# Splitting each stage of a fused attention and expert kernel into steps per engine, and placing all steps with a list scheduler

## The chip, the cores and the metric

The kernel runs on one core of a Trainium2 chip. The metric is the device time of one execution in microseconds (us); lower is better. Every time given is a median unless it says otherwise. Times inside an execution are counted from the start of the profiled span and come from one profiled execution of each kernel.

In this kernel TensorE does all matrix products and transposes and writes them into PSUM, an on-chip memory used as eight banks. VectorE and ScalarE work on the results; copying a result out of PSUM is called an *eviction*. GpSimd issues the loads. The *granted clock* is the share of its full clock that the profile shows for TensorE; *half clock* means 0.5.

## The reference

Sliding-window causal attention (window 64) over 8 batches, 8 heads, 576 positions, head size 64. Then each batch is averaged over its positions, a gate picks one of 8 experts from the average, and the whole batch goes through that expert's two matrices.

```
scores = (1/sqrt(D)) * q @ k.T            # masked to 0 <= i - j < 64
attn   = exp(scores - max) / sum
x      = (attn @ v), heads side by side   # (8, 576, 512)
pooled = x.mean(axis=1);  e = argmax(pooled @ w_gate)
h      = relu(x @ w1[e])                  # 512 -> 1024
out    = gate_weight * (h @ w2[e])        # 1024 -> 512
```

One consequence governs everything: the expert of a batch is not known before all of that batch's attention is done. Its 4.2 MB of weights (float32 in memory, half that once loaded) can only be asked for after that.

## The kernel before

A batch is five *units*: units 0 to 3 are two heads each over positions 0 to 511, unit 4 is the last 64 positions of all heads. Units are numbered through, so units 0 to 4 are batch 0 and units 5 to 9 batch 1. The expert part of a batch is 18 *chunks*: nine of the first matrix and nine of the second. A string fixes the order in which stages are emitted; each engine then works through its own instructions in that order and waits for what it needs. The stages of a unit (cuts marked `# ...`):

```python
"Q1 L1 t1 T0 T1 U0 S0 U1 E0 S1 K0 T2 U2 S2 T3 E1 M K1 V0 U3 A0 E2 T4 K2 A1 X0 F2 U4 A2 "
"S3 L2 Q2 X1 S4 X2 E3 E4 K3 A3 K4 T5 A4 F2 X3 U5 X4 G0 H0 T6 V1 S5 F4 t2 U6 I0 E5 Q3 K5 "   # ...
"T11 X8 U11 A9 S10 t3 X9 E10 K10 C2 L3 C2 G1 Q4 V2 H1 I1 S11 C1 T12 E11 U12 A10 K11 X10 "   # ...

load_qk(0, 2, 4); load_v(0); load_qk(0, 4, 8); load_tail(0)     # first loads (heads from, to)

def unit_tp(b, i):   # T: 16 transposes of q and k into one PSUM bank (tp)              TensorE
def unit_te(b, i):   # U: copy of q, then copy of k, out of that bank (qt, kT)          VectorE
def unit_s(b, i):    # S: scores into PSUM (s); units 1-4 first add the mask by matmul  TensorE
def unit_e(b, i):    # E: pe = exp(scale * s)                                           ScalarE
def unit_k(b, i):    # K: pe *= mask (not for units 1-4)                                VectorE
def unit_a(b, i):    # A: denominators, products and reciprocals in one stage
    lb = ps_a.tile([128, 4, 128], FP32, tag="lb")
    for hh in range(2):
        nc.tensor.matmul(out=lb[...], lhsT=ones, rhs=pe[:, hh], ...)      # denominators
    for m in range(8):
        for hh in range(2):
            nc.tensor.matmul(out=av[...], lhsT=vt[:, m, 2*i+hh], rhs=pe[:, hh, m], ...)
    nc.scalar.activation(out=ln, in_=lb, func=AF.Ln)
    nc.scalar.activation(out=rl, in_=ln, func=AF.Exp, scale=-1.0)         # 1/denominator
def unit_x(b, i):    # X: x = av * rl, and its sum over positions                       VectorE
def shift_v(b):      # V: v moved between partition halves (batch 0: half of it on ScalarE)
def gate1(b):        # G: gate matmul (gps), argmax, loads of the expert's w1 and w2
def w1_chunk(b, ft): # C: four matmuls into ph, and at once relu(gate*ph) out of PSUM
    relu(hm[:, ft], ph, gates[b], RM[ft])        # RM = 'adadadada': ScalarE, VectorE in turn
def w2_chunk(b, r, half):                        # C: po, copied out by WM = 'adad'
# Q, L, t: loads of q and k, of v, of the last 64 rows.  F: filler matmuls.
```

All loads go through one in-order queue, so the letters Q, L, t and G also fix the order of loads. PSUM is full: one bank for transposes, two for scores, one each for denominators and products, three for expert chunks (which, before the first chunk, units 1 and 3 of batch 0 may use for transposes and products, and unit 4 for products).

The softmax here doesn't subtract the row's maximum and nothing guards it: scores larger than these inputs give would overflow.

Of the kernel before, what the change touches and what calls it, by code (L numbers as in the profile page):

```python
# [1 line left out]
TB=1;MB=3;KM='d';RM='adadadada';WM='adad'  # L2
WU=12;PB={int(c) for c in '1.2.3.4'.split('.')};KA={int(c) for c in ''.split('.') if c};KK={int(c) for c in ''.split('.') if c};VA={int(c) for c in '0'.split('.') if c};  # L3
OPS = (
    "Q1 L1 t1 T0 T1 U0 S0 U1 E0 S1 K0 T2 U2 S2 T3 E1 M K1 V0 U3 A0 E2 T4 K2 A1 X0 F2 U4 A2 "
    "S3 L2 Q2 X1 S4 X2 E3 E4 K3 A3 K4 T5 A4 F2 X3 U5 X4 G0 H0 T6 V1 S5 F4 t2 U6 I0 E5 Q3 K5 "
    "T7 U7 A5 S6 E6 X5 K6 T8 A6 S7 T9 U8 S8 E7 K7 E8 X6 A7 U9 S9 X7 T10 K8 E9 A8 U10 C1 K9 "
    "T11 X8 U11 A9 S10 t3 X9 E10 K10 C2 L3 C2 G1 Q4 V2 H1 I1 S11 C1 T12 E11 U12 A10 K11 X10 "
    "C3 T13 A11 S12 E12 C2 U13 K12 C1 T14 X11 U14 A12 S13 E13 C3 T15 K13 X12 A13 U15 X13 C1 "
    "S14 E14 K14 C2 T16 A14 S15 U16 E15 X14 C2 K15 C3 t4 G2 H2 L4 Q5 V3 I2 S16 C1 T17 E16 "  # L10
    "U17 A15 K16 X15 C3 T18 A16 S17 E17 C2 U18 K17 C1 T19 X16 U19 A17 S18 E18 C3 T20 K18 "
    "X17 A18 U20 X18 C1 S19 E19 K19 C2 T21 A19 S20 U21 E20 X19 C2 K20 C3 t5 G3 H3 L5 Q6 V4 "
    "I3 S21 C1 T22 E21 U22 A20 K21 X20 C3 T23 A21 S22 E22 C2 U23 K22 C1 T24 X21 U24 A22 S23 "
    "E23 C3 T25 K23 X22 A23 U25 X23 C1 S24 E24 K24 C2 T26 A24 S25 U26 E25 X24 C2 K25 C3 t6 "
    "G4 H4 L6 Q7 V5 I4 S26 C1 T27 E26 U27 A25 K26 X25 C3 T28 A26 S27 E27 C2 U28 K27 C1 T29 "
    "X26 U29 A27 S28 E28 C3 T30 K28 X27 A28 U30 X28 C1 S29 E29 K29 C2 T31 A29 S30 U31 E30 "
    "X29 C2 K30 C3 t7 G5 H5 L7 V6 I5 S31 C1 T32 E31 U32 A30 K31 X30 C3 T33 A31 S32 E32 C2 "
    "U33 K32 C1 T34 X31 U34 A32 S33 E33 C3 T35 K33 X32 A33 U35 X33 C1 S34 E34 K34 C2 T36 "
    "A34 S35 U36 E35 X34 C2 K35 C3 G6 H6 V7 I6 S36 C1 T37 E36 U37 A35 K36 X35 C3 T38 A36 "
    "S37 E37 C2 U38 K37 C1 T39 X36 U39 A37 S38 E38 C3 K38 X37 A38 X38 C1 S39 E39 K39 C2 A39 "  # L20
    "X39 C5 G7 H7 I7 C31 "
# [19 lines left out]
def kernel(  # L41
# [70 lines left out]
    def shift_v(b):  # L112
        vt = vw[b % NV]
        (nc.scalar.copy if b in VA else nc.vector.tensor_copy)(  # L114
            out=vt[64:128, 0:8:2], in_=vt[0:64, 1:9:2])
        nc.vector.tensor_copy(out=vt[0:64, 2:9:2], in_=vt[64:128, 1:9:2])
# [32 lines left out]
    load_qk(0, 2, 4)  # L149
    load_v(0)  # L150
    load_qk(0, 4, 8)
    load_tail(0)
# [31 lines left out]
    def unit_t(b, i):  # L184
        unit_tp(b, i)
        unit_te(b, i)

    def unit_tp(b, i):
        qm, km, qkt = qkv[b]
        if i < NP:  # L190
            if b == 0 and i % 2:
                tp = ps_m.tile([128, 2, 4, 128], BF16, tag="mo", name="tp")
            else:
                tp = ps_t.tile([128, 2, 4, 128], BF16, tag="tp", name="tp")
# [13 lines left out]
    def unit_te(b, i):  # L208
        tp = tps.pop((b, i))
        if i < NP:  # L210
            qt = apool.tile([128, 8, 64], BF16, tag="qt", name="qt", bufs=3)
            (nc.scalar.copy if b * NU + i in KA else nc.vector.tensor_copy)(  # L212
                out=qt.rearrange("q m (r p) -> q m r p", r=4),
                in_=tp[:, 0].rearrange("q r (m p) -> q m r p", p=16))
            (nc.scalar.copy if b * NU + i in KK else nc.vector.tensor_copy)(
                out=kT[b % 2][:, i, 64:64 + SM].rearrange("q (p r) -> q p r", r=4),
                in_=tp[:, 1].rearrange("q r p -> q p r"))
            tT[b, i] = qt
        else:
            qt = apool.tile([128, NP, 64], BF16, tag="qtt", name="qtt")  # L220
            nc.vector.tensor_copy(out=qt, in_=tp[:, :, 0:64])
            nc.vector.tensor_copy(out=kT[b % 2][:, :, 64 + SM:64 + S], in_=tp[:, :, 64:128])
            tT[b, i] = qt

    def unit_s(b, i):
        qt = tT.pop((b, i))
        kt = kT[b % 2]
        pm = b * NU + i in PB
        sp = ps_s.tile([128, 2, 512], FP32, tag="s", name="s")
        if i < NP:  # L230
            if pm:
                for hh in range(2):
                    nc.tensor.matmul(out=sp[:, hh], lhsT=ident, rhs=maskb,
                                     start=True, stop=False, skip_group_check=True)
            for m in range(8):
                for hh in range(2):
                    p0 = 64 * hh
                    nc.tensor.matmul(out=sp[:, hh, ts(m, 64)],  # L238
                                     lhsT=kt[p0:p0 + 64, i, 64 * m:64 * m + 128],
                                     rhs=qt[p0:p0 + 64, m], start=not pm, stop=True,  # L240
                                     skip_group_check=True)
        else:
            if pm:
                for hh in range(2):
                    nc.tensor.matmul(out=sp[:, hh, 0:256], lhsT=ident, rhs=masktb,
                                     start=True, stop=False, skip_group_check=True)
            for n in range(NP):
                for hh in range(2):
                    p0 = 64 * hh
                    nc.tensor.matmul(out=sp[:, hh, ts(n, 64)],  # L250
                                     lhsT=kt[p0:p0 + 64, n, SM:SM + 128],
                                     rhs=qt[p0:p0 + 64, n], start=not pm, stop=True,
                                     skip_group_check=True)
        sps[b, i] = sp

    def unit_e(b, i):
        sp = sps.pop((b, i))
        if i < NP:
            pe = apool.tile([128, 2, 8, 64], FP16, tag="pe", name="pe", bufs=4)
            nc.scalar.activation(out=pe.rearrange("c h m t -> c h (m t)"), in_=sp,  # L260
                                 func=AF.Exp, scale=scale)
        else:
            pe = apool.tile([128, 2, NP, 64], FP16, tag="pp", name="pp")
            nc.scalar.activation(out=pe.rearrange("c h n t -> c h (n t)"), in_=sp[:, :, 0:256],
                                 func=AF.Exp, scale=scale)
        pt[b, i] = pe

    def unit_k(b, i):
        if b * NU + i not in PB:
            pe = pt[b, i]  # L270
            nc.vector.tensor_tensor(out=pe, in0=pe, in1=mask if i < NP else maskt, op=ALU.mult)  # L271
# [3 lines left out]
    def unit_a(b, i):  # L275
# [5 lines left out]
        xm, xt = xs[b]  # L281
        if i < NP:
            pe = pt.pop((b, i))
            ab = (ps_m, "mo") if b == 0 and i % 2 else (ps_a, "av")
            av = ab[0].tile([128, 4, 128], FP32, tag=ab[1], name="av")
            lb = ps_a.tile([128, 4, 128], FP32, tag="lb", name="lb")
            for hh in range(2):
                p0 = 64 * hh
                nc.tensor.matmul(out=lb[p0:p0 + 64].rearrange("q r (m p) -> q m r p", p=16),  # L289
                                 lhsT=ones,  # L290
                                 rhs=pe[:, hh].rearrange("c m (r p) -> c m r p", r=4),
                                 start=True, stop=True, skip_group_check=True)
# [6 lines left out]
            ln = apool.tile([128, SM], FP32, tag="ln", name="ln")  # L299
            rl = apool.tile([128, SM], FP32, tag="rl", name="rl")  # L300
            nc.scalar.activation(out=ln, in_=lb.rearrange("q r p -> q (r p)"), func=AF.Ln)  # L301
            nc.scalar.activation(out=rl, in_=ln, func=AF.Exp, scale=-1.0)  # L302
            avs[b, i] = (av, rl)
        else:
            pp = pt.pop((b, i))
            ab = (ps_m, "mo") if b == 0 else (ps_a, "av")
            al = ab[0].tile([128, 2, NP, 64], FP32, tag=ab[1], name="al")
            for hh in range(2):
                p0 = 64 * hh
                nc.tensor.matmul(out=al[p0:p0 + 64, 1], lhsT=ones, rhs=pp[:, hh],  # L310
                                 start=True, stop=False, skip_group_check=True)
            for n in range(NP):
                for hh in range(2):
                    p0 = 64 * hh
                    nc.tensor.matmul(out=al[p0:p0 + 64, 0, n], lhsT=vt[:, 8, 2 * n + hh],
                                     rhs=pp[:, hh, n],
                                     start=False, stop=(n == NP - 1), skip_group_check=True)
            ln = apool.tile([128, NP, 64], FP32, tag="lnt", name="lnt")
            rl = apool.tile([128, NP, 64], FP32, tag="rlt", name="rlt")
            nc.scalar.activation(out=ln, in_=al[:, 1], func=AF.Ln)  # L320
# [139 lines left out]
    def chunk(x):  # L460
        for _ in range(x):
            todo.pop(0)()
# [46 lines left out]
```

## Time and profile before

| | before |
|---|---|
| time, median (range) | 229.66 us (229.13 to 230.75) |
| profiled span | 228.0 us |
| first gate matmul / second | 31.5 / 54.1 us |
| first expert matmul | 47.3 us |
| last matmul group starts | 222.5 us |

The page of the profile, busy totals and the rows over 40 equal slices of 5.7 us (a digit is the busy share of a slice in tenths; PEclk is the clock granted to TensorE, in tenths):

```profile
span 228.0 us, 6537 instructions
...
PE 201.7 (88%) x2748; PEld 114.5 (50%) x2748; DVE 140.9 (62%) x387; ACT 122.0 (54%) x194; POOL 82.0 (36%) x109
...
PE   7419656789999999999999999999999999999792
...
DVE  4406378578768785769577958786678755514211
ACT  2233843856765576557746675567656674422320
...
PEclk9955988769999999999999999999999999999998
```

From the tenth slice to the fourth from the end TensorE is at 9. Before that it is mostly below (the 9 in the fourth slice is at half clock), and the granted clock sinks again and again.

The windows view of the kernel before: for each stretch its length, then busy time and instruction count of TensorE, of its weight loads, of VectorE, ScalarE and GpSimd, then the granted clock:

```profile
core 0: us, PE busy (x) PEld busy (x) DVE busy (x) ACT busy (x) POOL busy (x), PEclk, DMA share, GB/s
23.00:30.00 7.00, 3.94 (x92) 2.48 (x92) 2.94 (x11) 5.74 (x11) 5.92 (x7) 1.00 2.28 146
30.00:40.00 10.00, 6.29 (x121) 4.00 (x122) 7.97 (x28) 3.58 (x7) 6.18 (x9) 0.83 1.36 173
40.00:50.00 10.00, 7.71 (x147) 4.85 (x141) 5.56 (x15) 6.67 (x10) 1.97 (x4) 0.66 1.37 199
77.60:101.10 23.50, 23.26 (x341) 13.49 (x341) 17.53 (x47) 14.82 (x25) 9.70 (x12) 1.00 1.32 185
```

In a full stage (the last line) TensorE works 23.26 of 23.5 us. Between 23 and 50 us it works 17.9 of 27 us, part of that filler and part at a lowered clock. VectorE and ScalarE aren't full there either (16.5 and 16.0 of 27 us): the engines wait for one another.

Marked moments of the timeline of TensorE before (start, duration, instruction, and in brackets how long the engine had been idle and what released it):

```profile
10.29 0.41 PE L238 MATMUL s<-qt,kT_97 64*128 64x64 bf16 x16
15.86 0.64 PE L199 MATMUL tp<-ident,qm 128*64 128x128 bf16 x8 [5.17 <-DMA qm<-in_q_dram]
...
31.48 0.41 PE L345 MATMUL gps<-gpr,ones_104 128*128 128x64 f32 x2 [2.62 <-DVE gpr L341]
...
36.15 0.41 PE L289 MATMUL lb<-pe,ones 128*64 128x512 f16 x2
...
39.54 0.41 PE L289 MATMUL lb<-pe,ones 128*64 128x512 f16 x2 [1.69 <-DVE pe L271]
...
42.93 0.64 PE L289 MATMUL lb<-pe,ones 128*64 128x512 f16 x2 [0.25 <-DVE pe L271]
...
46.28 0.64 PE L289 MATMUL lb<-pe,ones 128*64 128x512 f16 x2 [0.78 <-DVE pe L271]
...
47.28 1.89 PE L400 MATMUL ph<-xm,w1t 128*128 128x512 f16 x4
```

The q rows of heads 4 to 7 arrive only at 15.9 us. The `lb` lines are the denominators of four successive units of batch 1; they come every 3.4 us. The last line is the first expert chunk.

What TensorE waited for in all, before (total us, times, longest):

```profile
PE tp L199 <- DMA qm<-in_q_dram: 5.6, 2, 5.2
PE lb L289 <- DVE pe L271: 2.7, 3, 1.7
PE gps L345 <- DVE gpr L341: 2.6, 1, 2.6
...
PE s L238 <- ACT pe L260: 1.2, 1, 1.2
...
PE po L422 <- DMA w2t<-in_moe_w_dram: 1.2, 1, 1.2
```

### The profile page before, as it was taken

The page shows a single profiled execution, that of the slowest core. Times are in us where ns is not written, and L with a number is a line of the kernel's source. Part 1 is how long each engine was busy: PE and PEld are TensorE (multiplying, and loading weights), DVE is VectorE, ACT ScalarE, POOL GpSimd, SP SyncE. Part 2 cuts the span into 40 slices and gives each one's busy share as a digit, 9 for nine tenths or more (in the row PEclk, how much of TensorE's full clock was granted, in tenths as well). Part 3 has the DMA queues.
Part 4 walks back from the last instruction along what each step waited for, and adds up shares of the span by engine and source line. Part 5 has one row for each costly group of instructions (what it writes and reads, how often), then busy time and mean ns, then how long its engine had stood idle before and what let it go on. Part 6 is the DMA issues. An engine that isn't in the chain of part 4 may idle for free.

```text
span 228.0 us, 6537 instructions
## 1 busy us (share of the span) xinstructions
PE 201.7 (88%) x2748; PEld 114.5 (50%) x2748; DVE 140.9 (62%) x387; ACT 122.0 (54%) x194; POOL 82.0 (36%) x109
## 2 busy tenths in 40 slices
PE   7419656789999999999999999999999999999792
PEld 2306433544656464646564655566464645545441
DVE  4406378578768785769577958786678755514211
ACT  2233843856765576557746675567656674422320
POOL 7995739324800094028412751265003000400000
PEclk9955988769999999999999999999999999999998
DMA  5999999999999989999999999999993995199523
GB/s 54 135 152 187 148 146 191 205 193 173 178 209 241 204 122 191 232 216 189 207 240 219 196 205 241 218 198 203 235 226 39 200 203 178 16 179 271 113 93 115
DMA packets 85870, 40.81 MB, mean 179 GB/s; under 512 B 47952, under 2 KB 81744, under 8 KB 85840
## 3 DMA queue, kind: packets, MB, share of 16 engines
q0 software_dynamic: 79424, 30.94, 113.6%
q1 hardware_dynamic: 6416, 9.46, 12.8%
q8 instruction: 21, 0.34, 0.6%
q14 instruction: 9, 0.07, 0.1%
HBM read 61.88 MB, written 9.44 MB: 313 GB/s over the span
## 4 chain that ended last, share of the span: by engine, by line
PE 45%; DMA 30%; DVE 9%; ACT 6%; POOL 4%; issue 3%; POOLq 0%; DVEq 0%
PE po L422 16%; PE ph L400 11%; DMA km<-in_k_dram 11%; DMA w2t<-in_moe_w_dram 8%; DMA vw_95<-in_v_dram 7%; DMA w1t<-in_moe_w_dram 4%; PE tp L199 4%; ACT pe L260 2%; PE av L296 2%; PE po L433 2%; PE lb L289 2%; PE s L238 2%; PE ph L407 2%; DVE hm L388 2%; ACT rl L302 2%
## 5 line engine op out<-in xcount | busy, mean ns | idle before, releaser
L422 PE MATMUL po<-w2t,hm 128*128 128x512 f16 x256 | 59.8, 380 | 1.2 <-DMA w2t<-in_moe_w_dram 1.2
L400 PE MATMUL ph<-xm,w1t 128*128 128x512 f16 x256 | 60.1, 384 | 0.2 <-DVE hm L388 0.2
L361 POOL DMA_DIRECT2D w1t<-in_moe_w_dram x16 | 12.3, 776 | 73.2 <-DVE vw_94 L114 21.6
L400 PEld LDWEIGHTS <-w1t 128*128 128x128 f16 x256 | 23.5, 99 | 26.8 <-issue 1.2
L260 ACT ACTIVATE pe<-s 128x1024 f16<-128x1024 f32 x32 | 32.2, 1008 | 8.1 <-PE s L238 8.1
L422 PEld LDWEIGHTS <-hm 128*128 128x128 f16 x256 | 22.9, 98 | 26.5 <-DMA w2t<-in_moe_w_dram 1.3
L386 ACT ACTIVATE hm<-ph,gw 128x512 f16<-128x512 f32 x32 | 22.0, 686 | 22.6 <-PE ph L400 22.4
L388 DVE TENSOR_SCALAR hm<-ph,gw 128x512 f16<-128x512 f32 x32 | 23.8, 745 | 11.3 <-PE ph L400 11.3
L301 ACT ACTIVATE ln<-lb 128x512 f32<-128x512 f32 x32 | 19.1, 596 | 18.8 <-PE lb L289 18.2
L328 DVE CUSTOM_DVE_ANT_0 xm<-av,rl 128x512 f16<-128x512 f32 x32 | 22.0, 687 | 11.3 <-ACT rl L302 7.9
L271 DVE TENSOR_TENSOR pe<-pe,mask 128x1024 f16<-128x1024 f16 x29 | 19.9, 688 | 11.0 <-ACT pe L260 11.0
L427 DVE COPY ob<-po 128x512 f32<-128x512 f32 x16 | 11.0, 689 | 21.8 <-PE po L422 21.8
L212 DVE COPY qt<-tp 128x512 bf16<-128x512 bf16 x32 | 13.5, 422 | 13.4 <-PE tp L199 13.3
L302 ACT ACTIVATE rl<-ln 128x512 f32<-128x512 f32 x32 | 20.1, 630 | 1.0
L199 PE MATMUL tp<-ident,qm 128*64 128x128 bf16 x256 | 13.9, 234 | 6.0 <-DMA qm<-in_q_dram 5.6
L427 ACT COPY ob<-po 128x512 f32<-128x512 f32 x16 | 9.4, 587 | 17.3 <-PE po L422 17.3
L289 PE MATMUL lb<-pe,ones 128*64 128x512 f16 x64 | 13.3, 409 | 3.5 <-DVE pe L271 2.7
L199 PEld LDWEIGHTS <-qm 128*64 128x64 bf16 x256 | 9.1, 115 | 13.8 <-DMA qm<-in_q_dram 5.9
L199 PE MATMUL tp<-ident,km 128*64 128x128 bf16 x256 | 13.4, 230 | 1.4 <-DMA km<-in_k_dram 1.4
L106 POOL DMA_DIRECT2D vw_94<-in_v_dram x12 | 10.6, 894 | 7.0 <-DMA qkt<-in_q_dram 4.4
L99 POOL DMA_DIRECT2D qkt<-in_q_dram x8 | 5.8, 720 | 19.6 <-DMA w2t<-in_moe_w_dram 19.6
L106 POOL DMA_DIRECT2D vw_95<-in_v_dram x12 | 10.7, 920 | 1.3 <-DMA km<-in_k_dram 1.3
(104 smaller groups left out, 271.0 us busy)
## 6 DMA issues: line engine op xcount, KB each, us to landing
w1t<-in_moe_w_dram POOLq DMA_DIRECT2D x16, 512.0 KB, 7.8
w2t<-in_moe_w_dram POOLq DMA_DIRECT2D x8, 1024.0 KB, 15.4
out_dram<-ob SPq DMA_DIRECT2D x32, 256.0 KB, 6.2
qm<-in_q_dram POOLq DMA_DIRECT2D x7, 512.0 KB, 17.2
km<-in_k_dram POOLq DMA_DIRECT2D x7, 512.0 KB, 17.4
vw_94<-in_v_dram POOLq DMA_DIRECT2D x12, 128.0 KB, 8.2
vw_95<-in_v_dram POOLq DMA_DIRECT2D x12, 128.0 KB, 15.6
vw_96<-in_v_dram POOLq DMA_DIRECT2D x8, 128.0 KB, 10.4
```

Source lines behind the costliest of these rows:

```text
L106: nc.gpsimd.dma_start(out=vt[:, 2 * J + 1], in_=v[b, :, 128 * J:128 * J + 128].rearrange("h c d -> c h d"))
L199: nc.tensor.transpose(tp[p0:p0 + 64, n, r], t[:, 2 * i + hh, ts(r, 64)], ident)
L260: nc.scalar.activation(out=pe.rearrange("c h m t -> c h (m t)"), in_=sp, func=AF.Exp, scale=scale)
L271: nc.vector.tensor_tensor(out=pe, in0=pe, in1=mask if i < NP else maskt, op=ALU.mult)
L301: nc.scalar.activation(out=ln, in_=lb.rearrange("q r p -> q (r p)"), func=AF.Ln)
L302: nc.scalar.activation(out=rl, in_=ln, func=AF.Exp, scale=-1.0)
L328: nc.vector.tensor_tensor_reduce(out=xm[:, i], in0=av.rearrange("q r p -> q (r p)"), in1=rl, scale=1.0, scalar=0.0, op0=ALU.mult, op1=ALU.add,
L386: nc.scalar.activation(out=o, in_=i, func=AF.Relu, scale=g)
L388: nc.vector.tensor_scalar(out=o, in0=i, scalar1=g, scalar2=0.0, op0=ALU.mult, op1=ALU.max)
L400: nc.tensor.matmul(out=ph, lhsT=w1t[:, kb, ts(ft, 128)], rhs=xm[:, kb], start=(kb == 0), stop=(kb == 3))
L422: nc.tensor.matmul(out=po, lhsT=hm[:, fb, ts(r, 128)], rhs=w2t[:, fb], start=(fb == 0), stop=(fb == 7))
L427: (nc.vector.tensor_copy if WM[r] == 'd' else nc.scalar.copy)(out=ob, in_=po)
```

## The change

Its intent: stages that use several engines are cut into one step per engine, so that a scheduler can place each step where its engine has room. Denominators (`l`), reciprocals (`R`) and products (`A`) become separate, as do the q copy (`U`), the k copy (`k`), the gate matmul (`g`) and the gate's choice (`G`), and every eviction of an expert chunk (`r`). Copies and evictions name their engine (`a` ScalarE, `d` VectorE). A list scheduler then made a new order of all steps; the order's text is replaced as a whole. The core of the diff:

```diff
-TB=1;MB=3;KM='d';RM='adadadada';WM='adad'
+TB=1;MB=3;LO='24.48.V.t';WU=12
-    "Q1 L1 t1 T0 T1 U0 S0 U1 E0 S1 K0 T2 U2 S2 T3 E1 M K1 V0 U3 A0 E2 T4 K2 A1 X0 F2 U4 A2 "
+    "Tm0 Tm1 Ua0 kd0 Sb0 Ua1 kd1 E0 Tm2 S1 Ua2 kd2 l0 E1 Q1 Tm3 R0 K1 S2 Ud3 kd3 L1 E2 l1 "
+    "V0 R1 S3 T4 K2 E3 Am0 M Ud4 kd4 l2 X0 S4 K3 Am1 R2 t1 Am2 X1 E4 l3 X2 R3 Am3 K4 Q2 F2 "
+    "Tm5 X3 l4 T6 Ua5 kd5 A4 R4 Tm7 Tm8 Ud6 Ua7 X4 S5 ka6 E5 kd7 g0 Ud8 ka8 K5 S6 G0 E6 F2 "
+    "T9 V1 l5 H0 S7 R5 I0 Ud9 Am5 kd9 K6 E7 X5 F3 l6 Am6 R6 K7 S8 L2 E8 X6 F2 l7 Am7 R7 "
     # ... (the rest of the order, old and new)
-    load_qk(0, 2, 4)
-    load_v(0)
-    load_qk(0, 4, 8)
-    load_tail(0)
+    for c in LO.split("."):       # q,k of heads 2-3, of heads 4-7, then v, then the tail
+        ...
-    def unit_a(b, i):             # denominators, products, reciprocals together
+    def unit_l(b, i):             # denominators: matmuls into lb
+    def unit_a(b, i, e):          # products: matmuls into av
+    def unit_r(b, i):             # reciprocals: Ln and Exp out of lb
-            relu(hm[:, ft], ph, gates[b], RM[ft])
+            evac.append(lambda e: relu(hm[:, ft], ph, gates[b], e))   # placed later by 'ra'/'rd'
```

Counted in the new order: 96 of 112 expert evictions are on ScalarE (56 before), 14 of 40 k copies and 9 of 40 q copies (none before). The masks of units 1 to 4 go back from a matmul to VectorE, unit 0 gets a matmul. Nine transposes and seven products now use expert banks (two and three before). In the queue of loads, v of batch 2 now comes behind q and k of batch 2 and the weights of batch 0, and v of batch 3 behind the weights of batch 1; before, each came ahead of them.

## The prediction

> What bounds the kernel now. The windows view splits the 228 us span into three parts. From about 57 us to 215 us TensorE is the bound: between 72 and 166 us a batch takes 23.5 us and TensorE is busy 23.26 of it, while VectorE has 17.5 and ScalarE 14.8 and the chain of waits is nearly all TensorE. Before 57 us TensorE is not full: from 17 to 60 us it is busy 33.3 of 43 us, some of that filler, at granted clocks of 0.59 to 0.83 in the stretches with gaps. It waits 5.2 us for the q rows of heads 4 to 7 (landed at 15.9 us, because v was loaded first), 2.6 us before the first gate matmul (31.5 us), and 1 to 1.7 us per unit of batch 1 for mask products and exponentials; five units there take 36.4 to 49.7 us, 3.3 us each, although VectorE has about 2.6 us of work a unit and ScalarE 2.3. At the end, 8 us of matmuls, an eviction and a store follow the last weights (215.5 us).
>
> What the change does. Matmul work stays, less three pre-mask pairs of about 0.4 us (units 1 to 4 lose theirs, unit 0 gains one). Counted in the new order: 96 of 112 expert evictions go to ScalarE (56 before), 14 of 40 k copies and 9 of 40 q copies too; v shift 0 and three more mask products go to VectorE. With 0.69 us a relu eviction, 0.59 an output eviction, 0.68 a k copy, VectorE falls from 141 to about 105 us and ScalarE rises from 122 to about 159. Denominators and products are split, and q heads 4 to 7 load before v; weights 0 come ahead of v of batch 2.
>
> Critical path. (1) Start: q/k of heads 4 to 7 should land near 11.5 us, v near 15.5. VectorE has about 12 us of work between v and the first gate: gate 0 near 28.5 us (31.5 before). (2) Batch 1: per unit, the work is shared at 2.4 us each; the stage between gates 0 and 1 holds 18.4 us ScalarE, 17.4 VectorE, 15.5 TensorE, against 22.6 us measured before, with two more expert chunks in it. Gate 1 near 49 us instead of 54. TensorE is full from about 42 us instead of 50 to 57: a lead of 7 to 9 us. (3) Steady stages cannot gain: TensorE is already 99% busy. They may lose 0.2 to 0.6 us each, because ScalarE now has about 21 of 23.5 us and output banks wait their turn there. (4) End: same work, same loads; about 0.
>
> The Trainium skill ("Perfetto Trace Analysis", Optimization Strategy) says that interleaving regimes with different most-contended engines may help; that is the gain here. "TensorE: Matmul & The Clock Gate", Part 1, says idleness gates the clock; the profile agrees (0.58 to 0.67 after gaps), so closing gaps should also recover 1 to 2 us.
>
> Sum: 229.7 - 9 + 1.5 = 222 us. Range 217 to 227. Faster by over 2%: 0.72, within 2%: 0.23, slower: 0.05.
>
> What would show it. First gate matmul at 27 to 30 us, second at 47 to 51; TensorE slices full from about 42 us; batch period still 23 to 24 us; last weights' landing about 8 us earlier; ScalarE busy near 159.
>
> What would make it wrong. TensorE waiting for ScalarE's evictions in each steady stage (period above 24.2 us); expert weights 0 landing after 42 us because loads, in flight all the time (DMA slices at 9), are the limit early; the shorter second expert stage outrunning its weights.

## The result

| | before | changed |
|---|---|---|
| time, median (range) | 229.66 us (229.13 to 230.75) | 217.88 us (217.61 to 218.27) |
| profiled span | 228.0 us | 215.7 us |
| gate matmuls 0, 1 | 31.5, 54.1 us | 26.1, 43.1 us |
| first expert matmul | 47.3 us | 35.4 us |
| gate matmul 7, chunks before it | 194.5 us, 113 | 182.6 us, 112 |
| busy VectorE / ScalarE | 140.9 / 122.0 us | 109.6 / 152.0 us |
| TensorE at half clock before 60 us | 20.4 us | 10.2 us |

The ratio is 0.9482, with a 95% interval of 0.9444 to 0.9521: faster by 5.2%.

The same lines of the page, changed kernel (slices of 5.4 us):

```profile
span 215.7 us, 6505 instructions
...
PE 200.8 (93%) x2743; PEld 110.1 (51%) x2743; DVE 109.6 (51%) x328; ACT 152.0 (70%) x256; POOL 83.5 (39%) x109
...
PE   7668789999999799999999999999999999999991
...
DVE  4259789875671548737673447543576263200000
ACT  2477789967798566975788678975887567636631
...
PEclk9965899999999999999999999999999999999998
```

TensorE's row is at 9 from the seventh slice on, with one 7, instead of from the tenth.

The windows view of the changed kernel, the same stretches and one full stage:

```profile
core 0: us, PE busy (x) PEld busy (x) DVE busy (x) ACT busy (x) POOL busy (x), PEclk, DMA share, GB/s
23.00:30.00 7.00, 5.38 (x140) 3.78 (x135) 6.17 (x25) 6.84 (x13) 2.31 (x4) 0.99 1.80 182
30.00:40.00 10.00, 9.87 (x218) 6.14 (x217) 8.96 (x21) 9.36 (x17) 6.79 (x9) 1.00 1.24 193
40.00:50.00 10.00, 10.00 (x112) 4.89 (x110) 7.30 (x26) 8.03 (x15) 5.49 (x7) 1.00 1.81 167
83.10:107.50 24.40, 23.78 (x343) 13.09 (x342) 15.66 (x43) 18.66 (x32) 9.84 (x12) 1.00 1.48 212
```

From 23 to 50 us TensorE now works 25.3 of 27 us, VectorE 22.4 and ScalarE 24.2. The engines overlap where they used to take turns.

Marked moments of TensorE's timeline, changed kernel:

```profile
10.07 0.41 PE L208 MATMUL tp<-ident,qm 128*64 128x128 bf16 x8 [0.46 <-DMA qm<-in_q_dram]
...
26.14 0.41 PE L360 MATMUL gps<-gpr,ones_104 128*128 128x64 f32 x2 [1.09 <-DVE gpr L356]
...
27.67 0.41 PE L291 MATMUL lb<-pe,ones 128*64 128x512 f16 x2
...
30.36 0.41 PE L291 MATMUL lb<-pe,ones 128*64 128x512 f16 x2
...
31.82 0.41 PE L291 MATMUL lb<-pe,ones 128*64 128x512 f16 x2
...
33.76 0.41 PE L291 MATMUL lb<-pe,ones 128*64 128x512 f16 x2
...
35.40 1.90 PE L420 MATMUL ph<-xm,w1t 128*128 128x512 f16 x8
```

The q rows of heads 4 to 7 arrive at 10.1 us, gate 0 comes at 26.1 us, the denominators of units 5 to 8 come 2.0 us apart on average instead of 3.4, and the first expert chunk starts at 35.4 us.

What TensorE waited for, changed kernel:

```profile
PE tp L208 <- DMA km<-in_k_dram: 2.2, 2, 1.2
...
PE gps L360 <- DVE gpr L356: 1.1, 1, 1.1
PE s L257 <- ACT pe L270: 1.0, 2, 0.7
...
PE av L313 <- DVE vw_94 L125: 0.8, 1, 0.8
PE av L313 <- DVE vw_94 L126: 0.5, 1, 0.5
PE tp L208 <- DMA qm<-in_q_dram: 0.5, 1, 0.5
```

No line of this answer says that TensorE waited for a ScalarE eviction.

Where the time came from, by the trace. At the first expert matmul, where neither kernel has done any expert chunk, the changed one is 11.9 us ahead: about 5.3 us of it at gate 0 and 6.5 us between gate 0 and that matmul. By then it has also done two sets of transposes and one of scores more, about 1.5 us of TensorE work at the durations of the full stages (0.57 and 0.34 us a set). At gate 2 the attention work done is equal, and the lead, less six chunks that the old kernel has done more, is about 13.8 us. From gate 2 to gate 7 the changed kernel does five chunks more (95 against 90, by the two orders) and takes 7.3 us more; at 0.90 us a chunk (an estimate from the chain of waits of the kernel before, where four chunks of the first matrix take 3.57 us and three of the second 2.70) that leaves a loss of about 2.8 us. TensorE's idle time between these gates is 2.7 us against 1.6: a wait of 1.35 us for v in one stage (at 72 us, the two `vw_94` lines above) is the largest piece. The rest fits more frequent changes of a matmul's shape on the array, the first pair of numbers in its line (`128*64` for transposes, denominators and products, `64*128` for scores, `128*128` for most chunks). Two denominator matmuls take 0.22 us directly behind work of their own shape, attention or expert, and 0.34 us behind another shape; between these gates the shape changes 111 times, against 84 before. At about 0.11 us a change, 27 more make 2.9 us, so this and the idle time are enough for the 2.8 us. The ends of matmuls are modelled in the profile, so that split of the loss is an estimate. At the end about 1.2 us comes back: the old kernel waits that long for its last weights, the new one does not. The two spans end 12.3 us apart.

### The profile page after: what moved, and what is told of

Its sections match the earlier page's. It is cut to its first block, busy times and chain, and to the rows that moved or that the text cites. A ratio compares the mean times of both kernels' runs of the same rounds, so it can differ in the third digit from the quotient of the medians.

```text
span 215.7 us, 6505 instructions
## 1 busy us (share of the span) xinstructions
PE 200.8 (93%) x2743; PEld 110.1 (51%) x2743; DVE 109.6 (51%) x328; ACT 152.0 (70%) x256; POOL 83.5 (39%) x109
## 4 chain that ended last, share of the span: by engine, by line
PE 42%; DMA 35%; POOL 7%; DVE 6%; issue 5%; ACT 2%; POOLq 1%; DVEq 0%
DMA w2t<-in_moe_w_dram 17%; PE po L454 15%; PE ph L420 12%; DMA vw_95<-in_v_dram 9%; DMA vw_96<-in_v_dram 6%; PE tp L208 3%; PE av L313 3%; DMA vw_94<-in_v_dram 3%; PE s L257 2%; PE lb L291 2%; PE po L462 2%; POOL qm L103 2%; PE ph L427 1%; POOL vw_94 L117 1%; POOL vw_95 L117 1%
## 5 line engine op out<-in xcount | busy, mean ns | idle before, releaser
L406 ACT ACTIVATE hm<-ph,gw 128x512 f16<-128x512 f32 x52 | 35.3, 685 | 9.4 <-PE ph L420 9.2
L420 PEld LDWEIGHTS <-w1t 128*128 128x128 f16 x256 | 23.3, 98 | 28.5 <-issue 3.5
L436 ACT COPY ob<-po 128x512 f32<-128x512 f32 x29 | 17.0, 586 | 19.5 <-PE po L454 19.5
L333 ACT ACTIVATE ln<-lb 128x512 f32<-128x512 f32 (+1 forms) x40 | 22.2, 556 | 5.1 <-PE lb L291 4.0
L334 ACT ACTIVATE rl<-ln 128x512 f32<-128x512 f32 (+1 forms) x40 | 23.5, 587 | 1.5 <-DVE pool L341 0.2
L380 POOL DMA_DIRECT2D w1t<-in_moe_w_dram x16 | 12.9, 813 | 27.7 <-PE ph L420 16.8
L103 POOL DMA_DIRECT2D qm<-in_q_dram x10 | 8.6, 862 | 33.2 <-DMA w2t<-in_moe_w_dram 19.4
L234 DVE COPY kT_97<-tp 128x512 bf16<-128x512 bf16 x14 | 9.6, 684 | 7.2 <-ACT qt L224 7.2
L110 POOL DMA_DIRECT2D qkt<-in_k_dram x8 | 5.5, 692 | 17.2 <-DMA w1t<-in_moe_w_dram 17.2
L224 ACT COPY qt<-tp 128x512 bf16<-128x512 bf16 x9 | 5.2, 583 | 9.2 <-PE tp L208 9.2
L224 DVE COPY qt<-tp 128x512 bf16<-128x512 bf16 x23 | 9.7, 422 | 3.6 <-PE tp L208 3.3
L117 POOL DMA_DIRECT2D vw_95<-in_v_dram x12 | 11.2, 951 | 0.5 <-DMA qm<-in_q_dram 0.5
```

What stands on the lines that cost most here:

```text
L117: nc.gpsimd.dma_start(out=vt[:, 2 * J + 1], in_=v[b, :, 128 * J:128 * J + 128].rearrange("h c d -> c h d"))
L333: nc.scalar.activation(out=ln, in_=lb[:, 0:n], func=AF.Ln)
L406: nc.scalar.activation(out=o, in_=i, func=AF.Relu, scale=g)
L420: nc.tensor.matmul(out=ph, lhsT=w1t[:, kb, ts(ft, 128)], rhs=xm[:, kb], start=(kb == 0), stop=(kb == 3))
L436: copy(e)(out=ob, in_=po)
```

## The experiments

Twelve kernels ran, all with correct results, each in three rounds against the kernel before on the same chip. There were three groups of rounds, on three chips, where the kernel before had medians of 229.58 to 229.95 us; the changed kernel was not run again in them, so differences from it are good to a few tenths of a microsecond at best. In the names, *old* and *new* mean before and changed. Where an old order had to run in the new code, each old stage was written as its steps, in the old sequence and with the old engines.

### The new order up to gate 1, the old order after it

```diff
 OPS: new order up to g1, with the loads t3 and L3 put in just before it
-     the remaining steps in the new order
+     the remaining steps in the old order, with the old engines
```

> The changed kernel's order up to the gate matmul of batch 1, the old order and old engines from there on. Theory (the whole gain is won before gate 1, 43 us against 54 us; steady stages and end give nothing): 217 to 219.5 us, gate 1 at 43 us, batch period about 23.5 us. Rival (the new order after gate 1 wins a good part, by fewer waits or by the ScalarE evictions): 222 us or more.

Measured: 223.28 us (222.51 to 224.35), ratio 0.9719. Neither number of the expectation. Gate 1 came at 42.5 us as it should, but the stage to gate 2 took 27.5 us. The timeline of TensorE of this run and its windows for that stage and the next say why:

```profile
47.25 0.32 PE L312 MATMUL av<-pe,vw 128*64 128x64 f16 x4 [4.42 <-DVE vw L124]
```

```profile
42.50:70.00 27.50, 22.51 (x255) 12.11 (x253) 14.70 (x41) 11.24 (x21) 13.33 (x16) 0.88 1.62 205
70.00:93.60 23.60, 23.25 (x340) 13.52 (x341) 17.47 (x47) 14.85 (x25) 9.71 (x12) 1.00 1.49 214
```

The old order asks for v of batch 2 directly after gate 1. The new queue loads it behind the weights of batch 0, so TensorE stood idle for 4.4 us and then ran part of the stage at half clock (0.88 on average). The next four stages take 23.6 to 23.9 us, like those of the kernel before. As a lead over the kernel before: 11.6 us at gate 1 (12.5 with the one chunk more that is done by then), 7.5 at gate 2, 6.6 at gate 7. The lead of the front is carried almost unchanged by the old order, less one loss made by mixing two orders that disagree about a load.

### The mirror image

```diff
 OPS: old order up to g1
-     the remaining steps in the old order
+     the remaining steps in the new order      (old first loads)
```

> The mirror image: old order, old load order and engines up to gate 1, the new order after it. Theory: 228 to 231 us, gate 1 at about 54 us. Rival: 226 us or less.

Measured: 231.13 us (230.35 to 231.68), ratio 1.0044, interval 0.9987 to 1.0102: the same as before. The first expert matmul is at 46.8 us. The new order of the full stages and of the end earns nothing when the front is old. Writing the old stages as separate steps hardly moved the first expert matmul either (47.3 us before). But gate 1 came at 58.8 us, not at the 54 us expected: by this hybrid's order, attention steps up to unit 13 stand ahead of it. By gate 2, at equal chunks (0.90 us each), it was 1.9 us behind the kernel before. So the seam cost something here too, and this run is not a clean test of the new full stages.

### The old order only after gate 2

> The new order up to the gate matmul of batch 2 (not of batch 1, as in the first try, which lost 6.7 us in the stage between gates 1 and 2 where it asked for v of batch 2 before it had landed), the old order and engines from there. Theory (from gate 2 on the new order gives nothing): 216.5 to 219.5 us. Rival (it gives something there): 221 us or more.

The edit is that of the first experiment with the cut at `g2`. Measured: 224.96 us (224.10 to 225.49), ratio 0.9781, interval 0.9733 to 0.9829 (so not clearly faster by 2%). This falls on the rival's side, but its cause is the same collision one batch later, now with v of batch 3. The timeline of TensorE of this run:

```profile
72.87 0.32 PE L312 MATMUL av<-pe,vw 128*64 128x64 f16 x4 [5.57 <-DVE vw L124]
```

The stage in which this lies takes 32.0 us instead of 23.5; the four stages from gate 3 to gate 7 take 23.6, 23.6, 23.6 and 22.8 us. In terms of lead at equal chunks: 12.8 us at gate 2, 4.3 at gate 3, 4.2 at gate 7. So from gate 3 on nothing is won or lost by which order runs. A hybrid free of the collision was not built, and a clean run of 218 us with the old order after the front is therefore not shown.

### Only the first loads in the old order

```diff
-LO='24.48.V.t'
+LO='24.V.48.t'
```

> The changed kernel with only the old order of the first loads (v before q and k of heads 4 to 7). Theory (the load order is what brings gate 0 forward): gate 0 at 29.5 to 31.5 us instead of 26.1, total 221 to 223 us. Rival (the order and engine split of the steps matter, the loads hardly): gate 0 within 1.5 us of 26.1, total under 219.5 us.

Measured: 221.78 us (221.34 to 222.25), ratio 0.9634. Gate 0 at 31.0 us, first expert matmul at 40.5 us. As the theory said: 3.9 us lost, and nearly the whole lead of gate 0 with it.

### Only the first loads in the new order, in the old kernel

```diff
     load_qk(0, 2, 4)
-    load_v(0)
     load_qk(0, 4, 8)
+    load_v(0)
```

> The old kernel with only the new order of the first loads. Theory: gate 0 falls from 31.5 to about 28 us and the total by 2 to 4 us, to 226 to 228 us; the rest of the 11.8 us needs the new order of steps. Rival (loads alone hardly matter): 229 us or more.

Measured: 228.37 us (228.00 to 228.52), ratio 0.9920. Gate 0 moves to 30.1 us only, and the gain is 1.6 us (against 229.95 us, the kernel before in the same rounds), below the range given. The old order places its first product ahead of the scores of unit 3, so late v holds it up: in this run TensorE waits 1.6 us for the first copy of v.

### v of batch 2 ahead of the weights of batch 0, as before

```diff
-  ... K4 Q2 F2 ... S8 L2 E8 ...
+  ... K4 L2 Q2 F2 ... S8 E8 ...
```

> The changed kernel with v of batch 2 loaded before q and k of batch 2 and weights 0, as in the old queue order. Theory (weights 0 ahead of v of batch 2 is what lets the experts start at 35 us): the first expert matmul waits for its weights until 38 to 41 us, total 219.5 to 222 us. Rival (weights would be there in time anyway): first expert matmul at 35 to 36 us, total within 1 us of 217.9 us.

Measured: 221.41 us (220.21 to 222.64), ratio 0.9647. Gate 0 is unmoved (25.8 us), and the first expert matmul comes at 39.8 us, 4.4 us later than in the changed kernel. The number fits the theory, its reason doesn't. What TensorE waits for in this run:

```profile
PE tp L207 <- DMA km<-in_k_dram: 4.2, 3, 2.2
PE tp L207 <- DMA qm<-in_q_dram: 1.9, 3, 0.9
```

It is q and k (2.2 and 0.5 us in the changed kernel); no line names the weights of the first matrix. The edit also puts v ahead of q and k of batch 2, whose transposes stand before the first expert chunk in the order of steps: TensorE stood idle for 0.9 us at 33.2 us and 2.2 us at 35.9 us for them, and then ran at half clock from 35.8 to 39.2 us. The first half of the first matrix landed at 38.4 us (35.2 in the changed kernel), so the weights would have held it up as well, but what they alone cost isn't shown. Later stages give a little back: the one after gate 2 takes 23.1 us instead of 24.7, since v is there in time.

### Both load orders, crossed with both orders of steps

> The new order of steps with both old load orders (v before q and k of heads 4 to 7; v of batch 2 before weights 0). If the two changes of loads add up (3.9 and 3.5 us alone): 224.5 to 226.5 us, so the order of steps alone is worth about 4 us of 11.8. If they overlap: 221.5 to 223.5 us.

> The old order of steps with both new load orders. The first alone gave 1.6 us. Theory (the loads pay only where the order of steps uses them, and the old order starts its experts after the eighth unit whatever the weights do): 227 to 229 us, first expert matmul still at 45 to 47 us. Rival (loads are worth 7 us by themselves): 224 us or less.

The edits are the load edits above, together, in the changed kernel and reversed in the old one. (The third difference in the queue, v of batch 3 behind the weights of batch 1, was not varied by itself.)

| | old loads | new loads |
|---|---|---|
| old order of steps | 229.66 us | 228.54 us (227.92 to 230.40), ratio 0.9936 |
| new order of steps | 221.42 us (219.37 to 222.28), ratio 0.9608 | 217.88 us |

The two load changes don't add up: each alone costs 3.5 to 3.9 us when undone, both together 3.5 us (by medians; the runs of the last kernel spread over 2.9 us). Either of them already puts the first expert matmul at 40 us, both at 42.2 us, and with v of batch 2 early the later stages run faster (23.1 us after gate 2). In the old order both are worth 1.1 us, its first expert matmul staying at 46.7 us (its profile is of the slowest of five executions). So of 11.8 us about 8.2 (7.6 to 10.4 by the interval of the ratio) belong to the order of steps without these changes of loads, and about 3.5 to loads that are worth only 1.1 us in the old order.

### The split of denominators undone

```diff
-  ... l5 H0 S7 R5 I0 Ud9 Am5 ...
+  ... H0 S7 I0 Ud9 l5 Am5 R5 ...        (all 40 units alike)
```

> The changed kernel with the split of denominators undone in all units: denominator matmuls directly ahead of the value product, logarithm and exponential directly behind it, the rest of the order untouched. Theory (reciprocals made early are part of the gain before gate 1, because the first products otherwise wait for v and then for two ScalarE steps): gate 0 at 27.5 to 29 us, total 219.5 to 222 us. Rival (the split is only book-keeping): total within 1 us of 217.9 us.

Measured: 232.13 us (229.89 to 232.63), ratio 1.0064: the whole gain is gone, far more than expected. The front explains 3.3 us of it (gate 0 at 29.0, first expert matmul at 38.7 us). The rest is lost in the stages that had been full: they take 25.8 to 28.2 us instead of 24.4 to 25.9. What TensorE waits for in this run:

```profile
PE s L256 <- DVE qtt L227: 3.5, 4, 1.0
PE av L312 <- DVE pool L340: 3.3, 6, 0.7
PE s L256 <- ACT kT L233: 2.8, 6, 0.6
PE s L256 <- ACT pe L269: 2.6, 5, 1.1
```

That fits late reciprocals: products then leave their single bank late (`pool` is the sum that the VectorE product writes), and ScalarE and VectorE reach the copies for the next scores late. The old kernel ran full stages of 23.5 us without the split, so the split is not shown to be a gain by itself; this order needs it.

### Evictions on the old engines

```diff
-  96 of 112 evictions 'ra'
+  evictions of each batch: a d a d a d a d a | a d a d | d, as before; places unchanged
```

> The changed kernel, all evictions of expert banks on the engines of before (56 of 112 on ScalarE instead of 96), order untouched. The prediction charged 1.5 us for the crowded ScalarE: then this should run at about 216.4 us. Rival (TensorE shows no wait for an eviction, the split of engines is worth nothing in the full stages): 217.2 to 218.6 us. If the ScalarE choice were itself part of the gain: 219 us or more.

Measured: 219.16 us (217.93 to 220.01), ratio 0.9530, interval 0.9479 to 0.9580, which overlaps that of the changed kernel. The median lies just inside the third expectation (219 us or more), the interval doesn't decide between it and the rival. Not faster, so the 1.5 us that the prediction charged for a crowded ScalarE does not show; whether the old engines cost up to 1 us is not settled.

### All q and k copies on VectorE

```diff
-  Ua0 Ua1 Ua2 Ua5 Ua7 ... ka6 ka8 ...
+  Ud0 Ud1 Ud2 Ud5 Ud7 ... kd6 kd8 ...
```

> The changed kernel with all q and k copies on VectorE again (9 and 14 were on ScalarE), order untouched. Up to gate 1 VectorE gets about 3.9 us more. Theory (before gate 1 VectorE and ScalarE together set the pace, sharing them is part of the gain): gate 1 at 45 to 47 us instead of 43.1, total 219.5 to 222 us. Rival (only the order counts): gate 1 within 1 us, total under 219 us.

Measured: 217.99 us (217.14 to 218.26), ratio 0.9473. The front is 1.3 us later (gate 1 at 44.4 us, first expert matmul at 36.7 us), and the time is the same: stages later on give it back (23.6 us after gate 2 instead of 24.7). Half clock lasted 6.8 us here instead of 10.2. The engine of the copies is no cause of the gain that these runs can show.

### An attempt to go further

```diff
-  S5 ... K5 ... S9 ... K9          Ua5 Ua7 ka6 ka8          F2 F3 F2
+  Sb5 ... Sb9 (mask by matmul)     Ud5 Ud7 kd6 kd8          (fillers dropped)
```

> An attempt to beat both: between 23 and 40 us VectorE (8.96 of 10 us) and ScalarE (9.36 of 10) set the pace and TensorE runs fillers. Units 5 to 9 get their mask from a matmul ahead of the scores (0.43 us of TensorE each) instead of a VectorE product of 0.69 us, the four ScalarE copies of units 5 to 8 go to VectorE, the later fillers are dropped. Theory: ScalarE loses 2.3 us and VectorE 1 us net, first expert matmul 1 to 2 us earlier, total 216 to 217.2 us. Rival (other waits take over, or weights 0 are not there yet): 217.5 us or more.

Measured: 217.52 us (216.97 to 218.00), ratio 0.9475, interval 0.9435 to 0.9515: at the edge of the rival and the same as the changed kernel. The windows view of this run, to be read against the lines of the changed kernel for the same stretches:

```profile
23.00:30.00 7.00, 4.82 (x111) 3.08 (x106) 6.84 (x27) 3.60 (x7) 2.14 (x3) 0.91 1.79 176
30.00:40.00 10.00, 9.77 (x208) 6.24 (x210) 6.52 (x18) 9.61 (x16) 7.56 (x10) 0.89 1.22 187
```

ScalarE was relieved as planned between 23 and 30 us (3.60 us busy instead of 6.84), but the first expert matmul came at 36.8 us, 1.4 us *later*. TensorE was busy 9.77 of the 10 us from 30 to 40 us, and its granted clock was at half from 28.8 to 32.2 us: work had been moved to an engine that ran slower there. That this is the reason is not shown, for two kernels with the same steps up to gate 1 as the changed one (the first and the third experiment) started their experts at 34.8 and 36.1 us: the front moves by about a microsecond from run to run. This was the only attempt, and it does not beat the changed kernel.

## Why the prediction was right, point by point

- *TensorE is the bound from 57 us on, not before; the gain is in the front.* Right. The lead is 11.9 us at the first expert matmul and 12.3 us at the end, after some 2 us more up to gate 2 and a net loss of about 1.5 us behind it; the old order carries such a lead on (from gate 3 on in the third experiment), and the new one behind an old front earns nothing (231.13 us).
- *Gate 0 near 28.5 us through the first loads.* Right in mechanism (undoing them puts gate 0 back to 31.0 us), too small in size: it came at 26.1 us. From the first copy of v (15.3 us) to gate 0 passed 10.8 us, not the estimated 13. VectorE was busy 9.1 us of them where the prediction had counted about 12 us of work.
- *Gate 1 near 49 us, TensorE full from 42 us, a lead of 7 to 9 us.* This is the mis-sized term: the front was worth 12 us and more. The prediction put 18.4 us of ScalarE work into the stage between the gates and about 20.5 us between them. The stage took 16.9 us, with ScalarE busy 16.2 us of it: less work than counted lay there, almost without bubbles, and expert chunks began at 35.4 us. The order of the queue, v of batch 2 behind its q and k and the weights of batch 0, was named (for the weights) but not costed; undoing it alone costs 3.5 us.
- *Steady stages lose 0.2 to 0.6 us each to ScalarE evictions.* The size was near by luck (about 2.8 us over five stages), the cause was wrong. TensorE shows no wait for an eviction, and giving them back to VectorE gains nothing. The trace shows late v and more changes of the matmuls' shape instead. About 1.2 us of the loss came back at the end. The forecast period of 23 to 24 us was missed too: gates 2 to 7 lie 24.4 to 25.9 us apart, with 17 to 22 chunks in a stage instead of 18.
- *Half clock: closing gaps recovers 1 to 2 us.* Half clock before 60 us fell from 20.4 to 10.2 us. No gain from it shows: the changed kernel and the two hybrids that share its steps up to gate 1 had 10.2, 6.8 and 6.8 us of half clock by then and reached gate 1 at 43.1, 42.5 and 43.8 us. Runs with much more of it (17.1 us in the two with the new steps and the old first loads) differ in other things too.
- *ScalarE near 159, VectorE near 105 us.* 152.0 and 109.6 us. A k copy takes ScalarE 0.59 us where VectorE's 0.68 had been charged; the rest of the two errors was not traced.

What stays open: which single moves inside the new order make up its 8.2 us. The runs show that the split of denominators is needed for it and that the engines of copies and evictions hardly matter. They don't tell the earlier transposes from the earlier reciprocals or from the earlier experts. Three more differences of the front were never varied alone: the use of the expert banks by nine transposes and seven products, the masks of units 1 to 4, and v of batch 3 behind the weights of batch 1.

## What to carry to other kernels

Look for the gain of a new order where engines take turns, and read it at one event before which both kernels have done nearly the same work, here the first expert matmul: once a single engine is full, an order carries a lead but doesn't make one. Loads and order of steps belong together: the same two load changes were worth 1.1 us in the old order and 3.5 in the new, and both hybrids with the new front stood still for a load that the old order wanted earlier. A step of a tight schedule can't be judged by undoing it alone: gluing the denominators back cost 14 us, in a schedule that had been built on their being apart.

## What the Trainium skill lacked or had wrong

- "TensorE: Matmul & The Clock Gate", Part 1, What's actually happening: it gives two states (4/8 and 8/8) and a window of 3413 ns. The runs agree: every stretch at lowered clock before the end was at 0.5 and lasted 3.4, 6.8, 10.2, 13.7 or 17.1 us. It does not say how busy a window must be, and the busy share of the profile doesn't tell either. Windows with TensorE busy 38% (8.3 to 11.7 us before), 51% (9.5 to 12.9 us changed) and 56% (25.4 to 28.8 us, mask by matmul) were followed by half clock, one with 68% (23.1 to 26.5 us changed) was not, but neither was one with 56% (10.3 to 13.7 us, old order after gate 2). Full clock came back after a window of 82% (24.4 to 27.8 us, old steps with both new loads) and not after one of 92% of the same run (41.4 to 44.8 us). These are shares of modelled busy time, from few windows.
- "Perfetto Trace Analysis", Identifying the Most-Contended Engine, warns that the busy share of matmuls is not a good measure of how close a kernel is to its bound. The runs agree: the stage after gate 3 is 97% busy in the changed kernel, yet a pair of denominator matmuls (`128*64`) takes 0.34 us directly behind a `128*128` or `64*128` matmul and 0.22 us behind one of its own shape (modelled ends).
- "TensorEngine Tiling (Array Packing)", Key Properties, gives no time for such a change of shape; here it was about 0.11 us, with 84 changes between gates 2 and 7 before and 111 after.
- "Perfetto Trace Analysis", Optimization Strategy, says that interleaving regimes may help. What it lacks is that an interleaved order and the order of loads have to be changed together (1.1 us against 3.5 us above).
